# Loading q, k and v in blocks of sixteen subtiles, with three buffers each, and k's squared norms back on TensorE

## The chip, the core and the metric

The kernel runs on one core of a Trainium2 chip. Five engines work side by side, each through its own instruction stream: PE (matrix multiplication), DVE (VectorE), ACT (ScalarE), POOL (GpSimd) and SP (SyncE, which here only starts DMAs). Sixteen DMA engines move data between HBM and the on-chip memory. The metric is the device time in microseconds of one launch; the median of three runs before the change is 270.2 us (270.14 to 270.89).

## What is computed

There are four batches of 6336 tokens with 256 channels each. Channel attention works over the channels: the Gram matrix of k and q over all tokens of a batch, with both normalized over the tokens, goes through a softmax, and v is multiplied by the result. A highway layer follows on the 25344 rows.

```python
B, N, C = (4, 6336, 256)
qn = q / (np.linalg.norm(q, axis=1, keepdims=True) + 1e-06)
kn = k / (np.linalg.norm(k, axis=1, keepdims=True) + 1e-06)
s = kn.transpose(0, 2, 1) @ qn / tau
s = s - s.max(-1, keepdims=True)
a = np.exp(s)
a /= a.sum(-1, keepdims=True) + 1e-09
x = (v @ a).reshape(B * N, C)
H = np.maximum(x @ w_h, 0.0)
T = 1.0 / (1.0 + np.exp(-(x @ w_t + b_t)))
out = (T * H + (1.0 - T) * x)
```

Inputs and output are float32 in HBM. The loads turn q, k and v into float16 on the way (so a byte written on chip stands for two bytes read), and the output is stored as float32.

## The kernel before

**Tiles.** Of a batch's 6336 rows, 48 subtiles of 128 rows are laid out so that each of the 128 partitions holds 48 successive rows; the 192 rows that remain are two subtiles of 96 rows, the tail. `CH = 8` subtiles make a chunk. A load brings one chunk of q, k or v: 8 subtiles, 8 KB in a row per partition in HBM (512 KB written on chip). There are six chunks and a tail per batch and input. `QK_BUFS = 5` and `V_BUFS = 5` tiles are kept for each of q, k and v. Output tiles also hold a chunk (`O_BUFS = 7`), and are stored a chunk at a time (1 MB).

**Stage 1** (`stage1`, lines 441 to 459) goes over a batch's subtiles of q and k. For each half of the channels it issues a 128x256 matmul k'q (line 453), a 128x128 matmul k'k (line 455) and a 128x128 matmul q'q (line 457); the diagonals of the last two are the squared norms. All add up in two PSUM banks, `sg0` and `sg1`. In batches 1 to 3, for the first `APART = 5` chunks of q and the first `APART_K = 1` chunk of k, the 128x128 matmul is left out (lines 454 and 456). There ACT squares the tile (`squares`, two instructions of four subtiles, line 472), POOL adds the squares up in three or four steps (`sum_squares`, lines 478 to 489), PE sums them over partitions (line 524), DVE copies the sums (line 528) and adds them to the diagonals (line 612).

**The chain** (`plan_chain`) follows stage 1 of a batch: diagonals on DVE (line 575), the power -0.5 on POOL (line 586), scaling, exponentials on ACT (line 652), transposes, and a product with the two weight matrices folded into it (line 698). It leaves the float16 matrices `mr`.

**Stage 2** goes over pairs of subtiles, 25 a batch and 100 in all, counted by g. A pair of v is transposed on PE (line 769, or line 763 in the last batch) and copied out by ACT or DVE (lines 539 and 541). Then come three products of four 128x256 matmuls each (line 809): h for the first layer, t for the gate, d for x. ACT takes relu (line 849) and tanh (line 863), copies the bias into t (line 539, or DVE at line 541), and DVE combines them (lines 870 and 889). In the last batch, from chunk `BY_DMA = 3` on, v is transposed by DMA instead, on SP's queue (`transpose_chunk`, line 777).

**Order.** No loop writes the instructions in order. Each piece of work is added as a task to `Plan` (lines 92 to 226) with an engine, a key, estimated costs and the tasks it depends on; `run` plays the tasks through and issues on each engine the ready task with the smallest key. So the order on each engine is fixed when the program is built, and the chip then follows it, waiting by semaphores. Keys are pair numbers g plus an offset by kind and stage from `PRIO`. Stage 1 of batch b+1 is spread over the pairs of batch b by `slot_of` with `HEAD` and `ENDS`. Loads are issued by POOL, in the fixed order of `seq` (lines 407 to 418), where `V_AHEAD` shifts those of v; a load is issued once a buffer is free, and POOL's additions go ahead of a load when both can go. `loads_stop` keeps loads off POOL while it is needed for the chain's power. At most eight loads are under way. Transposes by DMA have the key g - `AHEAD`.

**Stores** go out by SP in chunks. A store is held until a later chunk, `LAG = 5` chunks on, has its first result (`plan_holds`, lines 930 to 940: a 1 KB DMA into `held_row` waits for that result and the store is queued behind it); from pair `UNTIL = 61` on they are not held.

The loads of batch 0's q and k come first: chunks 0 to 3 whole, chunk 4 in two halves, chunk 5 in pieces of 4, 2 and 2 subtiles. The first chunk of batch 1, the weights and the first chunk of v follow.

```python
def drops(nm, b, s):
    if s < S and s % CH == CH - 1:
        return [(ld[(nm, b, s // CH)][0], nm)]
```

This is what gives a load's tile back: its last subtile's use.

Of the kernel before, what the change touches and what calls it, by code (L numbers as in the profile page):

```python
# [16 lines left out]
CH = 8  # L17
QK_BUFS = 5
V_BUFS = 5
O_BUFS = 7  # L20
LAG = 5
UNTIL = 61
AHEAD = 16
# [4 lines left out]
APART_K = 1  # L28
V_AHEAD = -3
# [3 lines left out]
    "tr": (-13.858, 5.164, -69.544, 4.416),  # L33
    "ev": (116.624, 56.093, 133.515, 109.473),
    "h": (-52.706, -43.549, -42.913, -10.323),
    "bias": (25.973, -17.497, 24.705, 39.419),
    "t": (22.848, -15.916, 56.403, 18.956),
    "relu": (-70.319, -81.16, 27.028, -53.997),
    "x": (-78.578, -45.936, -122.371, -23.396),
    "gate": (-39.338, -48.519, -69.153, -40.842),  # L40
    "prod": (16.639, 6.587, 21.565, -25.923),
    "res": (-18.603, 23.463, -13.022, -57.01),
    "s1": (92.914, 52.821, 130.881),
    "sq": (-18.222, 44.489, 8.075),
}
POW = 0.75
HEAD = 6
TAIL = 63
EV = BIAS = ("ACT", "DVE")
ENDS = [20.75, 51.5, 67.25]  # L50
# [179 lines left out]
def kernel(  # L230
# [19 lines left out]
    NJ = S // CH  # L250
    TR = (N - P * S) // 2
# [16 lines left out]
        "sqq": 2, "sqk": 2, "vT": 3, "vT_t": 1, "o": O_BUFS, "ot": 1, "uu": 3, "pp": 3, "vtsb": 9, "mr0": 2, "mr1": 2,  # L268
# [49 lines left out]
    def load(nm, b, j, s, n):  # L318
        src = src_of[nm][b]
        if j == NJ:  # L320
            t = new(f"tail_{nm}", [P, 2, C], f16, f"{nm}{b}_t")
            tiles[(nm, b, j)] = t
            nc.gpsimd.dma_start(out=t[0:TR, :, :], in_=tail_rows(src))
            return
        if s == 0:
            tiles[(nm, b, j)] = new(nm, [P, CH, C], f16, f"{nm}{b}_{j}")
        t = tiles[(nm, b, j)]
        nc.gpsimd.dma_start(  # L328
            out=t[:, s : s + n, :], in_=main_rows(src)[:, j * CH + s : j * CH + s + n, :]
        )  # L330

    def sub(nm, b, s):

        if s < S:
            return tiles[(nm, b, s // CH)][:, s % CH, :]
        return tiles[(nm, b, NJ)][0:TR, s - S, :]
# [6 lines left out]
    def plan_load(nm, b, j, s=0, n=CH):  # L343

        size = P * n * C * 4 if j < NJ else TR * 2 * C * 4
        tag = nm if j < NJ else f"tail_{nm}"
        x = plan.add(
            "POOL", len(plan.tasks), 0.54, 0, [], lambda: load(nm, b, j, s, n),
            take=[tag] if s == 0 else [], size=size * (1 if j < NJ and n > 2 else SHORT),
        )  # L350
        ld.setdefault((nm, b, j), []).append(x)
        x.first = s

    def loaded(nm, b, s):

        if s >= S:
            return [ld[(nm, b, NJ)][0]]
        return [[x for x in ld[(nm, b, s // CH)] if x.first <= s % CH][-1]]

    def drops(nm, b, s):  # L360

        if s < S and s % CH == CH - 1:
            return [(ld[(nm, b, s // CH)][0], nm)]
        if s == NS - 1:
            return [(ld[(nm, b, NJ)][0], f"tail_{nm}")]
        return []

    plan_load("q", 0, 0)
    plan_load("k", 0, 0)
    consts = plan.add("POOL", len(plan.tasks), 0.6, 1.5, [], constants)  # L370
    consts.serial = True
    for j in range(1, NJ - 2):
        plan_load("q", 0, j)
        plan_load("k", 0, j)
        if j == 2:
            for nm in "qk":
                plan_load(nm, 0, NJ)
            b_ld = [
                plan.add("POOL", len(plan.tasks), 0.54, 0, [], lambda u=u: load_b(u), size=4000)
                for u in range(2)  # L380
            ]
    for j, s, n in ((NJ - 2, 0, 4), (NJ - 2, 4, 4), (NJ - 1, 0, 4), (NJ - 1, 4, 2), (NJ - 1, 6, 2)):
        plan_load("q", 0, j, s, n)
        plan_load("k", 0, j, s, n)
# [11 lines left out]
    plan_load("v", 0, 0)  # L396
# [11 lines left out]
    for b in range(B):  # L408
        for j in range(NJ + 1):
            if (b, j) != (0, 0):  # L410
                seq.append((NP * b + CH // 2 * j - V_AHEAD, 1, "v", b, j))
            if b >= 1 and (b, j) != (1, 0):
                at = slot_of((b - 1) * NS + CH * j)
                seq.append((at, 0, "q", b, j))
                seq.append((at, 0, "k", b, j))
    seq.sort(key=lambda x: (x[0], x[1]))
    for _, _, nm, b, j in seq:
        plan_load(nm, b, j)
# [4 lines left out]
    def natural(b):  # L423

        return b == B - 1 and BY_DMA <= NJ
# [5 lines left out]
    def order_of(b):  # L431

        if b:
            return list(range(NS))
        return [*range(3 * CH), *range(S, NS), *range(3 * CH, S)]
# [5 lines left out]
    def stage1(b, s):  # L441
# [8 lines left out]
        for c in range(2):  # L450
# [3 lines left out]
            if not apart("k", b, s // CH):  # L454
                nc.tensor.matmul(sg[c][:, C : C + P], kc, kc, start=False, stop=False)  # L455
            if not apart("q", b, s // CH):
# [6 lines left out]
    def apart(nm, b, j):  # L463
        return b > 0 and j < {"q": APART, "k": APART_K}[nm]
# [4 lines left out]
    def squares(nm, b, j, half):  # L469
        sq_t[nm, b, j, half] = sq = new("sq" + nm, [P, CH // 2, C], f32, f"sq{nm}{b}_{j}_{half}")  # L470
        x = tiles[(nm, b, j)][:, half * CH // 2 : (half + 1) * CH // 2, :]
        nc.scalar.activation(out=sq, in_=x, func=Act.Square)  # L472

    def sum_squares(nm, b, j, step):
        add = partial(nc.gpsimd.tensor_tensor, op=AluOp.add)
        if step == 0:
            sq, other = sq_t[nm, b, j, 0], sq_t.pop((nm, b, j, 1))
            add(out=sq, in0=sq, in1=other)  # L478
        elif step == 1:
            sq = sq_t[nm, b, j, 0]  # L480
            add(out=sq[:, 0:2, :], in0=sq[:, 0:2, :], in1=sq[:, 2:4, :])
        else:
            sq = sq_t.pop((nm, b, j, 0))
            if j == 0:
                sums[nm, b] = small.tile([P, C], f32, tag=f"sums{nm}", name=f"sums{nm}{b}")
                add(out=sums[nm, b], in0=sq[:, 0, :], in1=sq[:, 1, :])
            else:
                add(out=sq[:, 0, :], in0=sq[:, 0, :], in1=sq[:, 1, :])
                add(out=sums[nm, b], in0=sums[nm, b], in1=sq[:, 0, :])

    def plan_squares(nm, b):

        ends, x = {}, None
        for j in range({"q": APART, "k": APART_K}[nm]):
            key = slot_of((b - 1) * NS + CH * j) + PRIO["sq"][b - 1] + (nm == "k")
# [3 lines left out]
                    "ACT", key, 0.97, 1.07, loaded(nm, b, CH * j + CH // 2 * n),  # L499
                    lambda j=j, n=n: squares(nm, b, j, n), take=["sq" + nm],  # L500
# [5 lines left out]
                "POOL", key, 2.36, 2.45, parts, lambda j=j: sum_squares(nm, b, j, 0), drop=[(parts[1], "sq" + nm)]  # L506
            )
            y = plan.add("POOL", key, 1.27, 1.35, [y], lambda j=j: sum_squares(nm, b, j, 1))
            x = plan.add(
                "POOL", key, 1.3 if j else 0.65, 1.4 if j else 0.75, [y] + ([x] if x else []),  # L510
                lambda j=j: sum_squares(nm, b, j, 2), drop=[(parts[0], "sq" + nm)],
# [3 lines left out]

        def over_partitions():
            sums[nm, b, "ps"] = ps = new("vt", [P, 2], f32, f"sumps{nm}{b}")
            for c in range(2):
                x = sums[nm, b]
                if nm == "q" or natural(b):  # L520
                    x = x[:, bass.ts(c, P)]
                else:
                    x = x.rearrange("p (w two) -> p two w", two=2)[:, c, :]
                nc.tensor.matmul(ps[:, c : c + 1], x, ones[:, 0:1], start=c == 0, stop=c == 1)

        def keep():
            sums[nm, b, "sb"] = sb = small.tile([P, 2], f32, tag=f"sumsb{nm}", name=f"sumsb{nm}{b}")
            nc.vector.tensor_copy(out=sb, in_=sums[nm, b, "ps"])
# [14 lines left out]
    def plan_chain(b, own, last, key, apart_sums):  # L543
# [65 lines left out]
        def rest_of(nm, n):  # L609
            if b:  # L610
                x = st["x"][:, n : n + 2]
                nc.vector.tensor_tensor(out=x, in0=x, in1=sums[nm, b, "sb"], op=AluOp.add)

        dq = dve(
            lambda: (diagonal(0), diagonal(1), rest_of("q", 0)), 0.9, 0.95, [last, consts] + apart_sums[:1]
        )
        nq = pool(lambda: norm(0), POW, POW + 0.2, [dq])
        dk = dve(
            lambda: (diagonal(2), diagonal(3), rest_of("k", 2)), 0.9 if b else 0.75, 0.95 if b else 0.8,
            [dq] + apart_sums[1:],  # L620
        )
# [149 lines left out]
    def transpose_chunk(b, j):  # L771
# [4 lines left out]
        src = tiles[("v", b, j)][0:nr, :, :].rearrange("p s c -> p (s c)")  # L776
# [168 lines left out]
    def plan_stage1(b):  # L945
        x, own = None, []
        part_ends, apart_sums = {"q": {}, "k": {}}, []
        if b:
            for nm in "qk":
                part_ends[nm], z = plan_squares(nm, b)  # L950
                apart_sums.append(z)
        for n, s in enumerate(order_of(b)):
            key = -100 + n if b == 0 else slot_of((b - 1) * NS + s) + PRIO["s1"][b - 1]
            deps = loaded("q", b, s) + loaded("k", b, s) + ([x] if x else [])
            away = [nm for nm in "qk" if apart(nm, b, s // CH)]
            x = plan.add(
                "PE", key, 0.44 - 0.11 * len(away), 0.66, deps, lambda s=s: stage1(b, s),
                take=[sg_tag(b, n)] if n < 2 else [],
                drop=[z for nm in "qk" if nm not in away for z in drops(nm, b, s)],
            )  # L960
            x.lat = x.pitch if n < NS - 1 else 0.66
            if s % CH == CH - 1:
                for nm in away:
                    plan.add("NONE", 0, 0, 0, [x] + part_ends[nm][s // CH], None, drop=drops(nm, b, s))
            if n < 2:
                own.append((x, sg_tag(b, n)))
        ready[b] = plan_chain(b, own, x, -50, apart_sums)
# [142 lines left out]
```

## Time and profile before

| | |
|---|---|
| median of three runs | 270.2 us (270.14 to 270.89) |
| profiled execution: its own time | 270.2 us |
| its span, first to last instruction | 268.4 us |
| mean granted TensorE clock | 0.993 |
| matmuls on PE | 2395 records |
| loads of q, k and v | 28, 28 and 24, and 12 of tails |
| HBM read and written | 78.38 MB and 25.95 MB |

A page gives busy time by engine, then 40 equal slices of the span (6.7 us each) with the busy share of each engine in tenths, the share of the DMA engines, and the rate in GB/s, counted in bytes written. PEclk is the granted clock in tenths. A chain of waits follows the last instruction back to what released it. Groups of instructions give line, engine, operation, operands and count, then busy time and the mean of one in ns, then the idle time of the engine before them and what ended it.

The rows that the change touches, from the groups by shape:

```profile
L455 PE MATMUL sg<-k 128*128 128x128 f16 x336 | 67.2, 222 | 0.0
L457 PE MATMUL sg<-q 128*128 128x128 f16 x144 | 32.0, 222 | 0.0
L472 ACT ACTIVATE sqk<-k 128x1024 f32<-128x1024 f16 x6 | 6.2, 1055 | 0.0
L478 POOL TENSOR_TENSOR sqk<-sqk,sqk 128x1024 f32<-128x1024 f32 x3 | 7.1, 2352 | 0.0
L481 POOL TENSOR_TENSOR sqk<-sqk 128x512 f32<-128x512 f32 x3 | 3.8, 1270 | 0.0
L486 POOL TENSOR_TENSOR sumsk<-sqk 128x256 f32<-128x256 f32 x3 | 2.2, 732 | 0.0
L524 PE MATMUL sumpsk<-ones,sumsk 128*128 128x1 f32 x12 | 1.6, 238 | 0.0
```

Matmuls are pipelined, so the 222 ns of one is its time through the engine and not the time between starts. The DMA issues, with KB written and the median time from issue to landing:

```profile
out_dram<-o SPq DMA_DIRECT2D x23, 1024.0 KB, 9.6
v<-in_v_dram POOLq DMA_DIRECT2D x24, 512.0 KB, 16.7
q<-in_q_dram POOLq DMA_DIRECT2D x21, 512.0 KB, 15.5
k<-in_k_dram POOLq DMA_DIRECT2D x21, 512.0 KB, 17.3
```

### The profile page before, as it was taken

To read this page: it belongs to the slowest core of one execution; us is meant where nothing else is said; L and a number is where in the kernel's file an instruction comes from. 1 tells how busy PE (TensorE), PEld (TensorE's weight loads), DVE (VectorE), ACT (ScalarE), POOL (GpSimd) and SP (SyncE) were. 2 spreads that over 40 slices of the span, in tenths; PEclk is the share of its full clock that TensorE was granted. 3 is DMA by queue.
4 is the path that set the end of the run, shared out by engine and by line. 5 is a ranking of instruction groups with operands and counts; after the bars stand their busy time and mean duration, and the time that the engine had idled before them with its cause. 6 is when DMAs were issued, how large, how long until landed. Compare 5 with 4: busy or idle time off the path is not lost.

```text
span 268.4 us, 6188 instructions
## 1 busy us (share of the span) xinstructions
PE 243.8 (91%) x2395; PEld 214.8 (80%) x2395; DVE 185.5 (69%) x392; ACT 198.3 (74%) x361; POOL 144.1 (54%) x176
## 2 busy tenths in 40 slices
PE   0687976999999999999999999999999999999990
PEld 0576853898999788999999789988898888888880
DVE  1000036637877887878867997886788988889993
ACT  1001018958978899889988898888879989999990
POOL 7233468997797456986587549976773000010000
PEclk9999999999999999999999999999999999999997
DMA  6999999999999999999999999999999999998994
GB/s 112 213 213 208 205 203 207 213 214 212 214 214 213 212 213 246 256 236 278 288 262 246 283 260 244 288 244 274 288 265 329 331 327 352 319 203 148 397 415 173
DMA packets 24527, 67.24 MB, mean 250 GB/s; under 512 B 9009, under 2 KB 11185, under 8 KB 21553
## 3 DMA queue, kind: packets, MB, share of 16 engines
q0 software_dynamic: 13472, 39.20, 74.7%
q1 hardware_dynamic: 11024, 27.64, 28.4%
q8 instruction: 19, 0.31, 0.4%
q14 instruction: 12, 0.09, 0.1%
HBM read 78.38 MB, written 25.95 MB: 389 GB/s over the span
## 4 chain that ended last, share of the span: by engine, by line
PE 75%; DMA 13%; DVE 4%; ACT 3%; POOL 2%; issue 1%; DVEq 0%; ACTq 0%; POOLq 0%
PE t L809 15%; PE h L809 15%; PE d L809 15%; PE sg L453 12%; DMA k<-in_k_dram 10%; PE vtps L769 6%; PE sg L455 6%; DMA v<-in_v_dram 2%; PE sg L457 2%; DVE pp L870 1%; PE t L840 1%; ACT uu L863 1%; ACT t L539 1%; DMA out_dram<-o 1%; PE ah L698 1%
## 5 line engine op out<-in xcount | busy, mean ns | idle before, releaser
L809 PEld LDWEIGHTS <-vtsb 128*128 128x128 f16 (+1 forms) x1044 | 99.7, 99 | 18.2 <-issue 5.0
L453 PE MATMUL sg<-q,k 128*128 128x256 f16 x384 | 79.3, 275 | 14.1 <-DMA k<-in_k_dram 14.1
L870 DVE SCALAR_TENSOR_TENSOR pp<-uu,d 128x512 f32<-128x512 f32 (+1 forms) x100 | 68.1, 683 | 26.0 <-PE d L809 13.4
L863 ACT ACTIVATE uu<-t 128x512 f32<-128x512 f32 (+1 forms) x100 | 59.4, 597 | 13.1 <-PE t L809 12.2
L455 PE MATMUL sg<-k 128*128 128x128 f16 x336 | 67.2, 222 | 0.0
L889 DVE SCALAR_TENSOR_TENSOR o<-h,pp 128x512 f32<-128x512 f32 x96 | 65.5, 685 | 1.5
L849 ACT ACTIVATE d<-h 128x512 f32<-128x512 f32 (+1 forms) x100 | 57.6, 581 | 6.3 <-PE h L809 4.9
L809 PE MATMUL t<-mr,vtsb 128*128 128x256 f16 (+1 forms) x348 | 52.0, 272 | 1.8 <-ACT t L539 1.7
L809 PE MATMUL h<-mr,vtsb 128*128 128x256 f16 (+1 forms) x348 | 52.1, 272 | 1.1 <-DVE vtsb L541 0.5
L453 PEld LDWEIGHTS <-k 128*128 128x128 f16 x384 | 37.7, 99 | 18.4 <-DMA k<-in_k_dram 15.5
L809 PE MATMUL d<-mr,vtsb 128*128 128x256 f16 (+1 forms) x348 | 51.8, 272 | 0.3 <-ACT d L849 0.2
L478 POOL TENSOR_TENSOR sqq<-sqq,sqq 128x1024 f32<-128x1024 f32 x15 | 35.5, 2364 | 20.5 <-ACT sqq L472 20.5
L539 ACT COPY t<-bias_all 128x512 f32<-128x512 f32 (+1 forms) x62 | 36.6, 590 | 1.5
L455 PEld LDWEIGHTS <-k 128*128 128x128 f16 x336 | 33.1, 99 | 0.9
L328 POOL DMA_DIRECT2D v<-in_v_dram x24 | 13.4, 559 | 35.6 <-DMA vT<-v 18.9
L457 PE MATMUL sg<-q 128*128 128x128 f16 x144 | 32.0, 222 | 0.0
L472 ACT ACTIVATE sqq<-q 128x1024 f32<-128x1024 f16 x30 | 31.0, 1051 | 0.0
L769 PE MATMUL vtps<-ident,v 128*128 128x128 f32 x144 | 27.7, 274 | 0.7 <-DMA v<-in_v_dram 0.7
L541 DVE COPY vtsb<-vtps 128x256 f32<-128x256 f32 (+2 forms) x55 | 22.9, 416 | 7.0 <-PE vtps L769 7.0
L575 DVE SCALAR_TENSOR_TENSOR junk<-sg,ident 128x128 f32<-128x128 f32 x16 | 4.6, 288 | 33.3 <-PE sg L457 32.7
L328 POOL DMA_DIRECT2D k<-in_k_dram x28 | 15.4, 549 | 9.6 <-DMA k<-in_k_dram 8.4
L328 POOL DMA_DIRECT2D q<-in_q_dram x28 | 15.6, 558 | 9.0 <-DMA q<-in_q_dram 7.3
(86 smaller groups left out, 267.7 us busy)
## 6 DMA issues: line engine op xcount, KB each, us to landing
out_dram<-o SPq DMA_DIRECT2D x23, 1024.0 KB, 9.6
v<-in_v_dram POOLq DMA_DIRECT2D x24, 512.0 KB, 16.7
q<-in_q_dram POOLq DMA_DIRECT2D x21, 512.0 KB, 15.5
k<-in_k_dram POOLq DMA_DIRECT2D x21, 512.0 KB, 17.3
q<-in_q_dram POOLq DMA_DIRECT2D x5, 256.0 KB, 9.8
k<-in_k_dram POOLq DMA_DIRECT2D x5, 256.0 KB, 9.1
out_dram<-o SPq DMA_DIRECT2D x2, 512.0 KB, 3.9
out_dram<-ot SPq DMA_DIRECT2D x4, 192.0 KB, 6.5
```

The source lines that it names most:

```text
L328: nc.gpsimd.dma_start(out=t[:, s : s + n, :], in_=main_rows(src)[:, j * CH + s : j * CH + s + n, :])
L453: nc.tensor.matmul(sg[c][:, 0:C], kc, qa, start=first, stop=False)
L455: nc.tensor.matmul(sg[c][:, C : C + P], kc, kc, start=False, stop=False)
L457: nc.tensor.matmul(sg[c][:, C + P : C + 2 * P], qa[:, cs], qa[:, cs], start=False, stop=last)
L478: add(out=sq, in0=sq, in1=other)
L539: nc.scalar.copy(out=out, in_=in_)
L769: nc.tensor.transpose(ps[:, u, 0:nr], v.bitcast(f32), ident0[0:nr, 0:nr])
L809: nc.tensor.matmul(out[0:nr, u, :], vt[u][kt][:, 0:nr], mr[kt][:, col * C : (col + 1) * C], **flags(u, kt))
L849: nc.scalar.activation(out=d[0:nr, :, :], in_=ps_t["h", b, i][0:nr, :, :], func=Act.Relu, scale=0.5)
L863: nc.scalar.activation(out=uu[0:nr, :, :], in_=ps_t.pop(("t", b, i))[0:nr, :, :], func=Act.Tanh, scale=-0.5)
L870: nc.vector.scalar_tensor_tensor(out=pp[0:nr, :, :], in0=el.pop(("uu", b, i))[0:nr, :, :], scalar=1.0, in1=ps_t.pop(("d", b, i))[0:nr, :, ...
L889: nc.vector.scalar_tensor_tensor(out=ot, in0=ps_t.pop(("h", b, i))[0:nr, :, :], scalar=0.0, in1=el.pop(("pp", b, i))[0:nr, :, :], op0=AluO ...
```

## The change

A load brings `LC = 16` subtiles, so a batch has three blocks and a tail per input, and each partition reads 16 KB in a row. There are three tiles for each of q, k and v. The work itself keeps its chunk of eight: sums of q's squares, output tiles, stores and transposes by DMA. A block's tile is given back when its sixteenth subtile has been used. Batch 0's q and k are still loaded eight subtiles at a time, up to the last block, which comes in pieces of 8, 4, 2 and 2; the first block of q and k of batch 1 comes as 4, 4 and 8, and that of v as 8 and 8. The tails of batch 0 are loaded and used after subtile 32, rather than 24.

The squares of k leave ACT and POOL: `APART_K` is gone, and line 455's matmul is issued for every subtile. q keeps its five chunks.

The numbers that place the work are others as well: `PRIO`, `HEAD`, `ENDS`, `UNTIL`, `AHEAD` and `V_AHEAD`. So the order on every engine changes. The counts that change on the engines: PE has 384 rather than 336 matmuls of k'k on whole subtiles, and 6 fewer sums over partitions. ACT has 6 squares fewer, 2 copies of `et`, 2 biases of the tail, 1 `mr` and 2 copies of `vtsb` more, which DVE has fewer. POOL issues 47 rather than 80 loads of q, k and v. SP has 11 rather than 10 holds.

```diff
 CH = 8
-QK_BUFS = 5
-V_BUFS = 5
+LC = 16
+QK_BUFS = 3
+V_BUFS = 3
 O_BUFS = 7
 LAG = 5
-UNTIL = 61
-AHEAD = 16
+UNTIL = 63
+AHEAD = 11
 BY_DMA = 3
...
 APART = 5
-APART_K = 1
-V_AHEAD = -3
+V_AHEAD = 2.5
...
-    "s1": (92.914, 52.821, 130.881),
-    "sq": (-18.222, 44.489, 8.075),
+    "s1": (2.894, 15.325, 6.393),
+    "sq": (-0.758, 4.066, 5.437),
 }
 POW = 0.75
-HEAD = 6
+HEAD = 4
 TAIL = 63
 EV = BIAS = ("ACT", "DVE")
-ENDS = [20.75, 51.5, 67.25]
+ENDS = [15.75, 46.75, 59.75]
...
+    NL = S // LC
...
         if s == 0:
-            tiles[(nm, b, j)] = new(nm, [P, CH, C], f16, f"{nm}{b}_{j}")
+            tiles[(nm, b, j)] = new(nm, [P, LC, C], f16, f"{nm}{b}_{j}")
         t = tiles[(nm, b, j)]
         nc.gpsimd.dma_start(
-            out=t[:, s : s + n, :], in_=main_rows(src)[:, j * CH + s : j * CH + s + n, :]
+            out=t[:, s : s + n, :], in_=main_rows(src)[:, j * LC + s : j * LC + s + n, :]
         )
...
-        if s < S and s % CH == CH - 1:
-            return [(ld[(nm, b, s // CH)][0], nm)]
+        if s < S and s % LC == LC - 1:
+            return [(ld[(nm, b, s // LC)][0], nm)]
...
+    for s, n in ((0, 8), (8, 4), (12, 2), (14, 2)):
+        plan_load("q", 0, NL - 1, s, n)
+        plan_load("k", 0, NL - 1, s, n)
...
-        return [*range(3 * CH), *range(S, NS), *range(3 * CH, S)]
+        return [*range(S - LC), *range(S, NS), *range(S - LC, S)]
...
-            if not apart("k", b, s // CH):
-                nc.tensor.matmul(sg[c][:, C : C + P], kc, kc, start=False, stop=False)
-            if not apart("q", b, s // CH):
+            nc.tensor.matmul(sg[c][:, C : C + P], kc, kc, start=False, stop=False)
+            if not apart(b, s // CH):
...
-        dk = dve(
-            lambda: (diagonal(2), diagonal(3), rest_of("k", 2)), 0.9 if b else 0.75, 0.95 if b else 0.8,
-            [dq] + apart_sums[1:],
-        )
+        dk = dve(lambda: (diagonal(2), diagonal(3)), 0.75, 0.8, [dq])
...
-        src = tiles[("v", b, j)][0:nr, :, :].rearrange("p s c -> p (s c)")
+        s = j * CH % LC
+        src = tiles[("v", b, j * CH // LC)][0:nr, s : s + n, :].rearrange("p s c -> p (s c)")
```

## The prediction

> **What bounds the kernel now.** I read the page, then the waits of PE, the timeline around first uses, and each load's landing.
>
> ```profile
> span 268.4 us, 6188 instructions
> ...
> PE 243.8 (91%) x2395; PEld 214.8 (80%) x2395; DVE 185.5 (69%) x392; ACT 198.3 (74%) x361; POOL 144.1 (54%) x176
> ...
> PE   0687976999999999999999999999999999999990
> ...
> DMA  6999999999999999999999999999999999998994
> GB/s 112 213 213 208 205 203 207 213 214 212 214 214 213 212 213 246 256 236 278 288 262 246 283 260 244 288 244 274 288 265 329 331 327 352 319 203 148 397 415 173
> ...
> PE 75%; DMA 13%; DVE 4%; ACT 3%; POOL 2%; issue 1%; DVEq 0%; ACTq 0%; POOLq 0%
> ```
>
> PE has almost no hole after 45 us, yet the DMA engines are full too, at 213 GB/s of float16 written until stores join at 101 us. Who waits?
>
> ```profile
> PE sg L453 <- DMA k<-in_k_dram: 14.1, 6, 8.9
> PE t L809 <- ACT t L539: 1.7, 4, 0.6
> PE vtps L769 <- DMA v<-in_v_dram: 0.7, 1, 0.7
> PE d L809 <- ACT d L849: 0.6, 2, 0.4
> PE h L809 <- DVE vtsb L541: 0.5, 1, 0.5
> PE h L809 <- DVE o L889: 0.5, 1, 0.5
> ```
>
> Columns: total, times, longest. The k waits lie in the first 41 us. Then PE waits 3.3 us for ACT and DVE. But PE meets its data just as they land:
>
> ```profile
> 62.42 0.27 PE L453 MATMUL sg<-q,k 128*128 128x256 f16 x1
> 62.53 0.22 PE L455 MATMUL sg<-k 128*128 128x128 f16 x1
> 62.59 0.27 PE L453 MATMUL sg<-q,k 128*128 128x256 f16 x1
> ```
>
> This is chunk 3 of batch 1; its k landed at 61.87 (the load's semaphore). The starts give pitches: 0.109 us for 256 columns, 0.056 for 128.
>
> I call the sum of pitches ahead of an instruction, in program order, its work position, and its start less that sum its lag. Lag grows only when PE idles. Before: 8.9 us at the first matmul, 20.6 at 62 us, 21.0 at 82, 22.4 at 128, 23.7 at 155, 25.0 at 183, 27.1 at the last. A load sets a floor under it: landing less position of first use. So far as 82 us the floors (k of chunks 1, 3 and 4: 49.54-30.0 = 19.5; 61.87-41.8 = 20.1; 69.43-49.0 = 20.4) lie within 0.6 us of the lag: DMA and PE bound together.
>
> **The change, part by part.** The sum is made against this execution, span 268.4, which is 270.2 us, 1.8 around it; the median is 270.2 too.
>
> *k's squares go back to PE.* 48 matmuls of 128x128 are added (8 subtiles x 2 halves x 3 batches): 48 x 0.056 = 2.7 us. The sums over partitions of k leave: the chain has q's twin at 0.46 us, three times 1.4. Net **+1.3 us**, all of it path, since nothing hides PE. Off go also 6 ACT squares (6 x 1.05 = 6.3 us) and three POOL chains (3 x 4.4 = 13 us). I count these as nothing: both engines have idle time (ACT 26%, POOL 46%). Bounds: -3.3, PE's waits on ACT and DVE, to 0; I take 0, since those waits (at 92, 151, 181 and 204 us) lie 12 us or more from any sum of k's squares (POOL's first steps start at 47, 106 and 163).
>
> *Loads of sixteen subtiles.* The bytes are the same; what moves is when a first use is allowed, since a whole load must land. The changed program's order gives positions. Its second q and k pair (subtiles 16 to 31 of batch 1) is first used at 39.6 us of work; its bytes have landed when, in the present kernel, chunk 3 has, as the same bytes stand ahead of both: 61.87. Floor 22.2, against 20.6 of lag now. Its third k is first used at 54.1 and ends with the bytes of chunk 5, 76.83: floor 22.8 against 20.9. v subtiles 32 to 47 of batch 0: first use 58.9; v chunk 5 landed at 87.65, less two tails and two k, q chunks now ahead of it (5.9), 81.75: floor 22.9 against 21.0. So PE loses 1.9 us here by waits for whole loads.
>
> *The larger row.* No load of this size is in the trace. Loads of 256 KB landed 1.24 us apart, of 512 KB 2.45: halving costs 1.2%. The packets' records, 327 ns for 4096 B and 173 for 2048, have 19 ns fixed, so 8192 B would be 2.9% quicker; the low bound is nothing gained, as 16 engines' packets overlap. I take 1.2%: six such loads by there, 29.4 us, give 0.35 (0 to 0.85). Lag **+1.5 us**. A rule speaks for much more: the Trainium skill, "DMA: Bandwidth & Descriptors", section "Anatomy of one DMA", gives each software-issued DMA 2.0 us fixed besides its bytes. There are 33 loads of q, k and v fewer, which would be 66 us. The row shows 512 KB loads landing 2.45 us apart, some six in flight (15.5 to 17.3 us from issue to landing), so the fixed part is hidden.
>
> *Does the lag stay?* Later floors: k of the last third of batch 2, first use 105.7, ends with bytes that landed at 130.4 (132.86 less one v chunk), less 0.6 for larger rows: 24.1, against 22.4+1.5. That adds **0.2**. v of batch 2, first use 132.0: 157.84-0.95-132.0 = 24.9 against 23.7+1.7, no more. k of the last third of batch 3, first use 159.5: (188.36-2.45-1.0)-159.5 = 25.4 against 25.0+1.7. Were the waits in between all taken up by the early one, this last floor would leave 0.4 of 1.7. With nothing from larger rows the early floor gives 1.9 and the one at 105.7 (24.7 against 24.3) 0.4 more. So 0.4 to 2.3.
>
> *Three buffers.* POOL issues loads in order past its sums; a load needs its tile free. The tightest early one, q of batch 2, needs q of batch 1 done at position 35.2, near 58 us, and its turn on the DMA comes at 82. Cover 24 us: nothing. v's last third of batch 3 waits for position 193.4, some 221 us, and is needed by transposes only.
>
> *Transposes by DMA move on SP's queue.* AHEAD falls from 16 to 11: the first, now issued at 222.2 and landed at 235.6, goes behind two stores that wait for pair 74 (near 230). By today's 13.4 us it lands at 243; PE wants it at position 217.9, lag 28.3: 246. Cover 3 us; if gone, it costs what it is late, and behind it are the stores of batch 3 on SP.
>
> *Tail.* Before, the last matmuls are d of pair 99, and DVE ends 2 us later. After, pair 98's d comes just ahead of them, so two more DVE operations (0.69 each), less the 0.44 and some overlap, stand behind: **+0.6** (0 to 1.2).
>
> Sum: 1.3 + 1.5 + 0.2 + 0.6 = 3.6; 270.2 + 3.6 = **273.8 us**. With the bounds of these terms and up to 1.5 us of new waits in the other order of ACT and DVE, its own range is 272.0 to 276.5.
>
> **Rivals.**
> *Lighter ACT and DVE take the later waits away* (faster). From 82 us on lag grows by 6.1 us, at the ends of batches' chains and in the last pairs. ACT has 6.3 us less to do. If over 4.4 of the 6.1 vanish, 273.8 falls under 269.4; all of it, with no floor, 267.7. Against: the floor of 25.4, worked out above, lets the end fall to 270.2+1.3+0.6-1.7 = 270.4, or 269 if rows are 2.9% quicker.
>
> *A new wait at the end* (slower still): the transposes, 3 us of cover, or v's 1 MB loads, which share the DMA with a later flush of stores (from pair 62 rather than 58). Each chunk late by 3 us gives 276.8. For: SP's order. Against: there is less load traffic left then than now, DMA falls to 203 GB/s and lower at 235 us.
>
> *The rows change nothing and the early floors are soft:* the lag of 1.7 us is taken up by waits that would have come anyhow, 270.2+1.3 and the last floor's 0.4 plus 0.6 of tail less today's waits of 1.5 on ACT: 271.0, no change.
>
> **How the numbers follow.** Forecast 0.69; slower by the end, 0.11; nothing, 0.10; faster, 0.10. What can be told from no change here is 0.3%, 0.8 us, so faster is under 269.4, slower over 271.0. The forecast and the late rival are slower: 0.80; 0.10 same, 0.10 faster. The range: the forecast's own, down to 270.4 where the last floor puts an end to absorption, and up to 277.8 for a chunk a little over 3 us late: 270.4 to 277.8.
>
> **What would show it.** PE waits on DMA for k and v between 55 and 85 us, where today are none; lag 22.5 rather than 21.0 at position 60; 1 MB loads landing 4.8 to 4.9 us apart; 384 matmuls of sg from k alone; PE's idle on ACT and DVE near 3 us still; transposes not waited for. I would be wrong if PE entered batch 1 at today's lag, if 1 MB loads landed under 4.76 apart, or if vT were waited for.

## The result, and the profile after

| | before | after |
|---|---|---|
| median | 270.2 us (270.14 to 270.89) | 273.6 us (273.38 to 274.37, four runs) |
| ratio to before, 95% interval | | 1.0125 [1.01, 1.0151] |
| profiled execution: its own time, its span | 270.2, 268.4 us | 273.5, 271.7 us |
| mean granted TensorE clock | 0.993 | 0.995 |

The kernel is slower by 3.4 us, where 3.6 was forecast (273.8). The page of the changed kernel, with the lines that answer to those of before:

```profile
span 271.7 us, 6186 instructions
...
PE 246.5 (91%) x2431; PEld 216.6 (80%) x2431; DVE 184.1 (68%) x379; ACT 196.1 (72%) x362; POOL 116.8 (43%) x138
...
PE 71%; DMA 13%; ACT 5%; DVE 5%; issue 2%; POOL 2%; DVEq 0%; ACTq 0%; POOLq 0%
...
L457 PE MATMUL sg<-k 128*128 128x128 f16 x384 | 75.7, 222 | 0.0
```

PE is busy 2.7 us longer in a span 3.3 us longer. POOL is relieved by 27 us and ACT by 2, and the kernel is slower all the same. In the chain of waits PE's share falls from 75% to 71%, and ACT and DVE together rise from 7% to 10%: PE now waits for others a little more. What it waits for (total, times, longest):

```profile
PE sg L456 <- DMA k<-in_k_dram: 13.5, 7, 8.9
PE t L806 <- ACT t L538: 1.5, 4, 0.8
PE vtps L765 <- DVE vtsb L540: 1.4, 2, 1.0
PE ah L694 <- DVE o L886: 0.6, 1, 0.6
PE d L806 <- ACT d L846: 0.5, 2, 0.3
```

The total for k is no larger than before (14.1), but two of its waits are new, and they lie behind 50 us, where before PE waited for no load at all. The timeline of PE in the changed kernel, with a few rows around them (start, duration, engine and line, tiles, shape, count, and in brackets the idle time before and what ended it):

```profile
50.03 0.28 PE L456 MATMUL sg<-q,k 128*128 128x256 f16 x1 [0.41 <-DMA k<-in_k_dram]
...
57.48 0.60 PE L806 MATMUL t<-mr,vtsb 128*128 128x256 f16 x4 [0.28 <-ACT t L538]
...
58.26 0.60 PE L806 MATMUL d<-mr,vtsb 128*128 128x256 f16 x4 [0.19 <-ACT d L846]
...
61.57 0.28 PE L456 MATMUL sg<-q,k 128*128 128x256 f16 x1 [0.54 <-DMA k<-in_k_dram]
```

Between 54.9 and 61.5 us PE has no stage 1 at all: the second block of k has not landed. It runs stage 2 alone, and there ACT does not keep up. Busy time by stretch shows it, first of the kernel before, then of the changed one (stretch, its length, busy us and instructions of PE, PE's weight loads, DVE, ACT and POOL, then clock, DMA share, GB/s):

```profile
55.00:60.00 5.00, 4.99 (x56) 4.46 (x54) 1.69 (x4) 1.69 (x4) 4.60 (x4) 1.00 1.05 211
60.00:65.00 5.00, 4.96 (x50) 4.33 (x48) 3.83 (x7) 4.72 (x8) 2.97 (x6) 1.00 1.07 215
```

```profile
55.00:60.00 5.00, 4.23 (x35) 3.16 (x34) 3.62 (x6) 4.49 (x10) 4.55 (x5) 1.00 1.04 218
60.00:65.00 5.00, 4.38 (x44) 3.61 (x43) 1.94 (x4) 4.19 (x7) 3.08 (x3) 1.00 1.04 216
```

PE loses 0.76 and 0.58 us here, and with them the lag of the prediction (start less work position) goes from 19.0 at position 30 to 22.9 at position 57, against 20.2 and 21.0 before. The last half microsecond of the 22.9 comes while PE runs stage 2 ahead of the third block of k, and not from a wait for it: the block landed at 76.19 us and is first used at 76.97.

```profile
75.03 0.38 PE L765 MATMUL vtps<-ident,v 128*128 128x128 f32 x2
75.47 0.60 PE L806 MATMUL t<-mr,vtsb 128*128 128x256 f16 x4
75.94 0.44 PE L765 MATMUL vtps<-ident,v 128*128 128x128 f32 x2
76.53 0.60 PE L806 MATMUL h<-mr,vtsb 128*128 128x256 f16 x4 [0.16 <-DVE o L886]
76.97 0.27 PE L456 MATMUL sg<-q,k 128*128 128x256 f16 x1
```

From start to start the two pairs of transposes take 0.44 and 0.59 us, where their pitches add up to 0.22; by the profile ACT's `t` ended the first delay and DVE's `o` the second. After position 57 the lag grows by 6.1 us to the last matmul in both kernels.

Position counts the added matmuls as work, so the wall clock must decide what they cost. Start of the first h matmul of the last pair of each batch, from PE's timeline:

| | before | after | difference |
|---|---|---|---|
| batch 0 | 109.53 | 111.39 | 1.86 |
| batch 1 | 170.04 | 172.19 | 2.15 |
| batch 2 | 223.02 | 225.85 | 2.83 |
| batch 3 | 260.60 | 264.10 | 3.50 |

More than half of the loss is there by the end of batch 0. The rest comes in small steps, in two traces whose orders differ.

### The profile page after: what moved, and what is told of

It reads as the page before. It is cut to its first block, busy times and chain, and to the rows that moved or that the text cites. A ratio compares the mean times of both kernels' runs of the same rounds, so it can differ in the third digit from the quotient of the medians.

```text
span 271.7 us, 6186 instructions
## 1 busy us (share of the span) xinstructions
PE 246.5 (91%) x2431; PEld 216.6 (80%) x2431; DVE 184.1 (68%) x379; ACT 196.1 (72%) x362; POOL 116.8 (43%) x138
## 4 chain that ended last, share of the span: by engine, by line
PE 71%; DMA 13%; ACT 5%; DVE 5%; issue 2%; POOL 2%; DVEq 0%; ACTq 0%; POOLq 0%
PE t L806 15%; PE h L806 14%; PE d L806 14%; DMA k<-in_k_dram 13%; PE sg L456 11%; PE sg L457 6%; PE vtps L765 5%; DVE pp L867 2%; PE sg L459 2%; ACT uu L860 2%; ACT sq L475 1%; ACT t L538 1%; PE t L837 1%; DVE o L886 1%; PE vtps L759 1%
## 5 line engine op out<-in xcount | busy, mean ns | idle before, releaser
L456 PE MATMUL sg<-q,k 128*128 128x256 f16 x384 | 81.8, 275 | 13.5 <-DMA k<-in_k_dram 13.5
L457 PE MATMUL sg<-k 128*128 128x128 f16 x384 | 75.7, 222 | 0.0
L846 ACT ACTIVATE d<-h 128x512 f32<-128x512 f32 (+1 forms) x100 | 58.2, 585 | 4.8 <-PE h L806 4.1
L456 PEld LDWEIGHTS <-k 128*128 128x128 f16 x384 | 37.8, 99 | 17.9 <-DMA k<-in_k_dram 15.3
L481 POOL TENSOR_TENSOR sq<-sq,sq 128x1024 f32<-128x1024 f32 x15 | 35.5, 2364 | 37.5 <-ACT sq L475 37.4
L538 ACT COPY t<-bias_all 128x512 f32<-128x512 f32 (+1 forms) x64 | 37.7, 590 | 1.6
L457 PEld LDWEIGHTS <-k 128*128 128x128 f16 x384 | 37.9, 99 | 1.1
L475 ACT ACTIVATE sq<-q 128x1024 f32<-128x1024 f16 x30 | 30.7, 1049 | 0.0
L540 DVE COPY vtsb<-vtps 128x256 f32<-128x256 f32 (+2 forms) x53 | 22.1, 418 | 7.3 <-PE vtps L765 6.7
L765 PEld LDWEIGHTS vtps<-ident,v 128*128 128x128 f32 x144 | 17.1, 141 | 3.9 <-DVE vtsb L540 2.3
L484 POOL TENSOR_TENSOR sq<-sq 128x512 f32<-128x512 f32 x15 | 19.2, 1282 | 0.9
```

What stands on the lines that cost most here:

```text
L456: nc.tensor.matmul(sg[c][:, 0:C], kc, qa, start=first, stop=False)
L475: nc.scalar.activation(out=sq, in_=qa, func=Act.Square)
L538: nc.scalar.copy(out=out, in_=in_)
L765: nc.tensor.transpose(ps[:, u, 0:nr], v.bitcast(f32), ident0[0:nr, 0:nr])
L846: nc.scalar.activation(out=d[0:nr, :, :], in_=ps_t["h", b, i][0:nr, :, :], func=Act.Relu, scale=0.5)
```

## Experiments

All ratios are to the kernel before, run on the same chip; its medians there were 270.76, 270.83 and 270.38 us. An edited kernel's line numbers are shifted by a few lines.

**1. The matmuls of k by k in the kernel before.** First the move of the squares alone, in the old order:

```diff
-            if not apart("k", b, s // CH):
+            if True:
                 nc.tensor.matmul(sg[c][:, C : C + P], kc, kc, start=False, stop=False)
     def squares(nm, b, j, half):
+        if nm == "k":
+            return
...
```

(and the same for POOL's sums of k, its sums over partitions and their copy).

> The kernel before, in its order, with k's squares of the first chunk on PE and its ACT squares, POOL sums and sums over partitions gone. If PE is the path: 48 x 0.056 - 3 x 0.46 = 1.3 us more, 271.5. If what ACT and POOL are spared shortens the waits after the softmax chains: under 271, down to 268.2 (PE's 3.3 us of waits on ACT and DVE).

Measured: 271.95 us, ratio 1.0044 [1.0029, 1.0058], which is 1.2 us (0.8 to 1.6), as the first term has it. Then the 48 matmuls with nothing taken away, so that only the first edit above is made:

> The kernel before in its own order with the same 48 matmuls added and nothing taken away (k's squared norms of batches 1 to 3 count the first chunk twice in the output). Moving the squares back to PE took 1.2 us there. If the matmuls count in full, as the prediction's first term has it, 2.7 us more than the kernel before, 272.9 on its 270.2. If a part of them fits into the waits ahead of the first chain (3.0 us for k's landings between positions 22.8 and 23.8), about 1.8.

Measured: 272.24 us, ratio 1.0071 [1.0057, 1.0084], 1.9 us (1.5 to 2.3) of the 2.7, near the second figure. In the trace, taken of a run of 272.62 us, less is hidden: the lag is 0.8 us under that of the kernel before at position 25, as the waits ahead of the first chain shrink, but only 0.3 at position 57 and 0.15 at the end. So most of this work counts here, and between 0.2 and 0.8 us of it does not.

**2. The same matmuls in the changed kernel.** Left out, in its own order (k's squared norms of batches 1 to 3 then lack the first eight subtiles):

```diff
-            nc.tensor.matmul(sg[c][:, C : C + P], kc, kc, start=False, stop=False)
+            if not (b and s < CH):
+                nc.tensor.matmul(sg[c][:, C : C + P], kc, kc, start=False, stop=False)
```

> The changed kernel, in its order, without the 128x128 matmuls k'k of the first eight subtiles of batches 1 to 3 (k's squared norms then miss those rows). If the added PE work is path from end to end, 48 x 0.056 = 2.7 us go: 273.6 - 2.7 = 270.9. If the landing of the second k block (61.5 us) sets PE's start there, the 16 matmuls ahead of it (0.9 us) only make PE wait longer: 271.8. If the added work was hidden: 273.6.

Measured: 273.81 us, ratio 1.0114 [1.0095, 1.0134]. The loss is 3.1 us (2.6 to 3.6), where that of the changed kernel is 3.4 (2.7 to 4.1). So 2.7 us less of work on PE gains nothing clear of noise, and 1.2 us at most. Then the same matmuls twice (`for _ in range(2 if b and s < CH else 1)` around the call):

> The changed kernel in its own order; each of the 48 matmuls of k by k that the change brought back (first eight subtiles of batches 1 to 3) is issued twice, so k's squared norms count that chunk twice in the output: 2.7 us more of PE work at the places where leaving it out gained nothing. If PE's work there is on the path, 2.7 us more, 276.3. If it lies in holes that landings and the chains of ACT and DVE leave, as leaving it out suggested, 1 us or less, 274.6 or below. Between the two: the holes were about filled by what the change added.

Measured: 274.32 us, ratio 1.0152 [1.013, 1.0174]: 2.7 us more of work cost some 0.7 (-0.2 to 1.6 by the intervals). So in the changed kernel these matmuls fill holes for the most part, and most of what they added is not on the path.

Where do the holes close? The waits of PE without the matmuls, then with twice the matmuls:

```profile
PE sg L456 <- DMA k<-in_k_dram: 12.4, 4, 8.9
PE t L807 <- ACT t L539: 1.8, 5, 0.8
PE cqb L634 <- DVE dcat L600: 1.4, 1, 1.4
PE vtps L766 <- DVE vtsb L541: 1.4, 2, 1.0
PE ah L695 <- DVE o L887: 0.9, 1, 0.9
```

```profile
PE sg L456 <- DMA k<-in_k_dram: 13.1, 6, 9.0
PE t L807 <- ACT t L539: 1.5, 4, 0.8
PE vtps L766 <- DVE vtsb L541: 1.4, 2, 1.0
```

The first eight subtiles of a batch are what PE does while the chain of the batch before runs on DVE, POOL and ACT. Without their k'k, PE stands longer for `dcat` and for DVE's work ahead of `ah`; with twice as much, neither wait is left (the rows not shown are of 0.5 us or less; the changed kernel itself stands 0.5 us for `dcat` and 0.6 for `ah`). Not all of the 1.4 us for `dcat`, in batch 0's chain, is due to the matmuls: in this execution the granted clock was 0.50 from 25.8 to 29.2 us, and three runs of the third experiment with such a drop and all their matmuls stood 0.98 us there. The drop does not hide a gain in the time: of the four runs two have a mean clock of 0.987 and two of 0.994 and 0.996, and all lie between 273.77 and 273.94 us. Batch 2's chain, in the stretch from 158 to 164 us: without the matmuls, in the changed kernel, and with twice as many.

```profile
158.00:164.00 6.00, 4.84 (x39) 3.69 (x38) 5.93 (x14) 3.96 (x11) 4.72 (x4) 1.00 1.03 249
```

```profile
158.00:164.00 6.00, 5.44 (x52) 4.57 (x51) 5.93 (x14) 4.28 (x12) 4.43 (x4) 1.00 1.02 246
```

```profile
158.00:164.00 6.00, 6.00 (x67) 5.59 (x65) 5.33 (x15) 4.07 (x11) 5.26 (x5) 1.00 1.04 239
```

In the first two DVE is full (5.93 of 6), and `ah` of batch 2 starts at 163.5 and 163.3 us: the added matmuls change PE's busy time and not the moment. Only in the third is PE itself full.

**3. What holds PE between 55 and 67 us.** Three things could: the landing of the second block of k, ACT, or the landing of v. First the block of k in two halves, with the order on PE, ACT and DVE kept; five later loads are issued a little behind their places, so that POOL's sums keep theirs:

```diff
+            for at in (0, CH) if (nm, b, j) == ("k", 1, 1) else (s,):
+                m = CH if (nm, b, j) == ("k", 1, 1) else n
                 nc.gpsimd.dma_start(
-                    out=t[:, s : s + n, :], in_=main_rows(src)[:, j * LC + s : j * LC + s + n, :]
+                    out=t[:, at : at + m, :], in_=main_rows(src)[:, j * LC + at : j * LC + at + m, :]
                 )
...
```

> The changed kernel with its own order on every engine but POOL; only the second block of k of batch 1 is loaded in two halves (ahead of it the block of q), and five later loads are issued a little behind their places so that POOL's sums keep theirs. Its first half then lands about 59.1 us instead of 61.5. Theory (the whole block of k is waited for, and the wait stays to the end): the 0.70 us wait of PE at 60.8 us goes, lag 22.2 instead of 22.9 at position 57, 272.9 us where the changed kernel takes 273.6. Rival 1 (the order laid around the late block sets the pace through ACT, and PE's wait for k only fills what ACT would take): the lag at position 57 falls by 0.3 or less. Rival 2 (what is won there is given back at later landings): lag 22.2 at position 57 and 273.6 us at the end.

Measured: 273.76 us, ratio 1.0108 [1.0083, 1.0133]. The half landed early, and PE's wait at 61.57 was gone: lag 21.1 at position 40. At position 45 it was 22.2 again, as in the changed kernel. The wait that took its place:

```profile
63.40 0.60 PE L820 MATMUL t<-mr,vtsb 128*128 128x256 f16 x4 [0.80 <-ACT t L552]
```

Then less work for ACT, with the block whole:

```diff
     def squares(b, j, half):
+        if (b, j) == (1, 1):
+            return
...
```

> The changed kernel in its own order; ScalarE's squares of the second chunk of q of batch 1 (2 x 1 us at 51.8 us) and GpSimd's four sums of them are left out, so q's squared norms of batch 1 lack one chunk in the output. Theory (the landing of the second block of k at 61.5 us is the floor): PE's 1.4 us of waits on ACT between 55 and 60 us go, PE then stands for k until 61.5 instead, about 2.1 us in place of 0.7, lag at position 57 still 22.9, 273.6 us. Rival (ACT's work sets the time in this stage): lag at position 57 1 us or more lower, 272.5 us or less.

Measured: 273.74 us, ratio 1.0108 [1.0081, 1.0135]. PE's waits for ACT's `t` fall to 0.1 us each, and it stands for k until 61.58 just the same; lag 22.9 at position 57, as the theory had it. But the wait for k was 0.56 us where 2.1 was expected: without ACT's waits PE had other short ones, for DVE's `t` and for ACT's `d`. Both edits:

> Both edits at once: the second block of k of batch 1 in two halves, and the squares of the second chunk of q of batch 1 with their sums left out (q's squared norms of batch 1 lack that chunk in the output). Theory: both causes of PE's holes between 55 and 61 us are gone, so lag 20.8 to 21.3 at position 57, as in the kernel before (21.0); if that is kept to the end, 271.6 us; if the later landings take it back, 273 us or more with lag back at 24 by position 105. Rival (neither was the cause): lag 22.5 or more at position 57.

Measured: 273.59 us, ratio 1.01 [1.0076, 1.0124], lag 22.8 at position 57: the rival, with the same 0.80 us for ACT at 63.41. ACT's squares of the third chunk stood at 59.7, ahead of the evictions that PE needed. So these went too:

> As the run with both edits (second block of k of batch 1 in two halves, squares of the second chunk of q of batch 1 left out), and ScalarE's squares of the third chunk of q of batch 1 (2 us at 59.7 us, ahead of the evictions that PE waited for at 63.4 us) with GpSimd's sums are left out too, so q's squared norms of batch 1 lack two chunks in the output. Theory (in a stretch of stage 2 alone, ScalarE paces PE, and its squares in that stretch are what PE stands for): the 0.8 us wait at 63.4 us goes, lag at position 45 21.2 to 21.4 instead of 22.1, and since waits early in the kernel are kept, 272.7 us. Rival (the next wait takes its place once more): lag at position 57 22.7 or more and 273.6 us.

Measured: 273.88 us, ratio 1.0124 [1.011, 1.0138], lag 22.8 at position 57. The rival once more. In this kernel PE waits for the next load:

```profile
66.89 0.44 PE L783 MATMUL vtps<-ident,v 128*128 128x128 f32 x2 [0.52 <-DMA v<-in_v_dram]
```

So three marks stand at nearly the same lag. In the changed kernel they are the landing of k's block, 61.52-39.6 = 21.9; the eviction that pair 6 waits for, 63.4-41.3 = 22.1; and the landing of v's second block, 66.41-44.8 = 21.6, or 22.0 in the last kernel, where it landed 0.4 us later. Taking one or two of them away shows the next one and gains nothing that lasts: the last pair of batch 0 stood at 111.39, 111.63, 111.38, 111.37 and 111.57 us in the changed kernel and these four. None of the four lifts v's mark, and the three with the split block set it later: v's second block landed at 66.89, 66.68 and 66.84 us, for a reason that was not looked for. So half a microsecond of gain by the first two marks may be hidden there; all three marks lie above 21.0, the lag before.

**4. A late landing alone.** In the kernel before, the second load of k of batch 1 was issued behind the third of q:

```diff
+        if (nm, b, j) == ("k", 1, 1):
+            return
+        for x, i in (("q", 2), ("k", 1)) if (nm, b, j) == ("q", 1, 2) else ((nm, j),):
...
```

> The kernel before in its own order; only the second load of k of batch 1 is issued behind the third of q instead of ahead of it, so that it lands about 2.45 us later, near 52.0 us, as a part of a longer load would. It is the landing floor by itself: wanted at position 30.0, floor 22.0 against a lag of 20.2, so PE waits about 1.8 us for it. Theory (a wait for a landing early in the kernel stays to the end, which is what the prediction's +1.5 rests on): 1.5 to 1.9 us more than the kernel before, 272.0 on its 270.2. Rival (the later growth of lag absorbs it): within 0.4 us of the kernel before.

Measured: 273.41 us, ratio 1.0096 [1.0062, 1.013], 2.6 us. The timeline of PE and its stretches show why it is more than 1.9:

```profile
52.82 0.28 PE L456 MATMUL sg<-q,k 128*128 128x256 f16 x1 [2.39 <-DMA k<-in_k_dram]
...
54.34 1.06 PE L812 MATMUL d<-mr,vtsb 128*128 128x256 f16 x4
```

```profile
53.00:54.00 1.00, 1.00 (x10) 0.83 (x9) 0.00 (x0) 0.00 (x1) 1.00 (x3) 0.74 1.07 213
54.00:55.00 1.00, 1.00 (x8) 0.76 (x7) 0.00 (x0) 0.97 (x2) 1.00 (x3) 0.50 1.04 209
55.00:56.00 1.00, 1.00 (x6) 0.74 (x5) 0.50 (x1) 0.22 (x1) 0.06 (x1) 0.50 1.11 221
56.00:58.00 2.00, 2.00 (x19) 1.68 (x16) 0.88 (x2) 1.72 (x3) 0.00 (x0) 0.78 1.05 213
```

The wait is 2.4 us, and half a microsecond later the granted clock falls to 0.50; a group of four matmuls takes 1.06 us, where the rows of the changed kernel above have 0.60. The clock costs 0.26+0.50+0.50+0.44 = 1.7 us more. In the trace, the lag is 4.3 us above that of the kernel before from position 34 on, and 4.3 at the last matmul: nothing of it is absorbed. The six runs lie at 272.6 to 272.7 (three) and 274.1 to 274.8 (three); the profiled one is of the second group, and 1.7 us between them is what the clock costs in the trace. That the first group kept its clock is an inference, as no trace of one was taken; the mean granted clocks of its runs, 0.992 to 0.998 against 0.986 to 0.991 in the second, speak for it. That group is 1.8 us over the kernel before, within the theory's 1.5 to 1.9.

**5. Smaller loads in place of whole blocks.** Every block of sixteen issued as two loads of eight, the changed kernel's order kept on PE, ACT and DVE:

```diff
+        if n == LC and nm == "q":
+            return
+        for at in (0, CH) if n == LC else (s,):
+            for x in "qk" if n == LC and nm == "k" else nm:
...
```

> The changed kernel with the same order on PE, ACT and DVE; only each load of sixteen subtiles is issued as two of eight, q and k in turns. If what PE loses is its waits for whole blocks, the wait for k at 60.8 us (0.7, and 0.25 just behind it) goes: 272.7. If all of the early lag (1.9 us) were such waits: 271.7. If block size has no part in it: 273.6, or more by eight to sixteen further issues on POOL (0.55 us each, off the path).

Measured: 291.76 us, ratio 1.0777 [1.0757, 1.0797]; none of the expectations. POOL's timeline:

```profile
54.68 0.53 POOL L333 DMA_DIRECT2D q<-in_q_dram  x1 [1.91 <-DMA q<-in_q_dram]
57.12 0.53 POOL L333 DMA_DIRECT2D k<-in_k_dram  x1 [1.92 <-DMA k<-in_k_dram]
57.66 2.35 POOL L486 TENSOR_TENSOR sq<-sq,sq 128x1024 f32<-128x1024 f32 x1
```

Most loads here are issued only when an earlier one has landed, and POOL stands 1.9 us in front of each. Its first sum of squares starts at 57.66 us, where the changed kernel has it at 45.12. Only two tiles hold squares, so ACT stands, and PE stood 13.7 us for ACT's `t`. The loads' issue, not their landing, made this time; it says nothing of the forecast's terms.

So the order was laid anew, with all loads of eight:

```diff
-            s = CH if (b, j) == (0, 0) else 0
-            seq.append((NP * b + (LC * j + s) // 2 - V_AHEAD, 1, "v", b, j, s))
+            for s in (0, CH) if j < NL else (0,):
+                if (b, j, s) != (0, 0, 0):
+                    seq.append((NP * b + (LC * j + s) // 2 - V_AHEAD, 1, "v", b, j, s))
...
```

> The changed kernel with tiles of sixteen, but loads of eight, each with its own due time, so that the order is laid anew with the same keys. If blocks cost mainly through the order (pairs of stage 2 in a row while a block is awaited, which ACT cannot keep up with: 1.4 us of waits on ACT at 55 to 60 us) and through the wait for k (0.9), lag at position 57 falls from 22.9 to about 21 and the time to 271.7. If the new keys are what costs, 273 or more.

Measured: 278.0 us, ratio 1.0267 [1.025, 1.0284]. The lag is 21.3 at position 57, 1.6 under the changed kernel's, as expected, and stays 1.3 to 3.3 under it up to position 180. The last pair of batch 0 comes at 110.63, 0.8 ahead of the changed kernel. From position 185 on it rises from 25.8 to 32.6 at the last matmul: another order of the last batch, in which PE waits in many small pieces. Then halves for batch 1's q and k and batch 0's v alone:

> The changed kernel's tiles, buffers and sort keys (v's lead 3 instead of 2.5), with loads of eight subtiles for q and k of batch 1 and v of batch 0 only, loads of sixteen after that, and the order laid anew by the planner. Theory (blocks of sixteen cost 1.6 us, all of it before position 57, because the work that a block feeds is ordered around its late landing): lag about 21.2 at position 57 and, if the planner's order of batches 2 and 3 is as good as the changed kernel's, 272.0 us. Rival (the order of the later batches decides by itself): lag 21.2 at position 57 and 273 us or more, with waits on ACT and DVE behind position 185.

Measured: 277.55 us, ratio 1.026 [1.0246, 1.0274]. Lag 21.4 at position 57, 25.8 at position 80, 33.2 at the end: the rival. The waits that did it lie at the end of batch 1's stage 1 and in the chain behind it:

```profile
91.62 0.60 PE L809 MATMUL t<-mr,vtsb 128*128 128x256 f16 x4 [0.87 <-ACT t L541]
...
96.68 0.67 PE L636 MATMUL cqb<-dcat,ones 128*128 128x256 f32 x2 [1.25 <-DVE inv L594]
```

Both laid a new order, from sort keys chosen for other loads. In both the early gain of smaller loads is there, and more than it is lost behind. No kernel of this study beat the kernel before.

## Why the prediction was right, and where not

*Blocks of sixteen, lag +1.5.* The place is right, and the mechanism in part. The second block of k landed at 61.52 us and was waited for; the working gave 61.87 less 0.35. But the 22.5 was the floor of two later loads, and these were not waited for: the third block of k landed at 76.19 and v's third at 81.05, floors of 22.1 and 22.2. The lag at position 57 to 60 is 22.9, 0.7 above any floor, and 1.9 above the kernel before where 1.5 was taken. The one landing that was waited for stands for 0.9 of this (21.9 against 21.0); the rest came behind it, from ACT and DVE at 63 and 75 to 77 us, which the forecast had only in its range. PE's two waits for k are a smaller part of it (0.9 us), because the order was laid around the late block and hands PE a stretch of stage 2 alone that ACT cannot feed. And it is not one mark but three within 0.5 us of lag: the third experiment removed two of them without gain. The fifth shows the size from the other side: with the same sort keys, loads of eight and the order they lead to, the lag there is 1.6 us less. Lifting v's mark, or all three, in the changed kernel's own order was not tried.

*k's squares, +1.3, "all of it path, since nothing hides PE".* This is the step that failed. In the kernel before it is right (1.2 us measured), and of the matmuls alone most counts. In the changed kernel it is wrong: the matmuls left out gain nothing clear of noise, doubled they cost some 0.7. They stand behind marks that are set in wall time, the landings up to 67 us and DVE's work at the batches' ends. Adding position and lag made the sum come out, since a lag under a fixed mark shrinks as position grows: with the matmuls left out the last lag is 32.0 rather than 29.0. So the blocks and their new order alone cost 3.1 of the 3.4 us (ratio 1.0114), and the two terms overlap instead of adding up. That the forecast fell within 0.2 us of the result is luck in part. In its own terms, too, errors offset each other: the lag of the last matmul is some 2 us above that before, where 1.7 was forecast, and the tail is 0.2 us shorter, where 0.6 longer was.

*Larger rows, 1.2%.* The six from 52 to 81 us landed 4.84 to 4.94 us apart, mean 4.88, against twice 2.45: 0.5%. The bound of nothing was nearer. That k's block landed just 0.35 us early, as worked out, is in part chance: the weights, ahead of any load of sixteen, had landed 0.29 us earlier than before (41.87 and 42.16). The profile counts 51 loads of q, k and v after, not 47, so 29 fewer than before and not 33. The Trainium skill ("DMA: Bandwidth & Descriptors", "Anatomy of one DMA") gives each software-issued DMA a fixed cost of about 2.0 us. Added up over 29 loads that would be 58 us, an estimate. The landings show none of it: split in two, k's block landed its halves 2.46 and 2.51 us apart.

*The floor at 105.7, +0.2.* It did not bind. Its load landed at 124.97 us, where the working had about 129.8: a floor of 19.3 against a lag of 24.1.

*ACT and POOL relieved, 0.* It fits the kernel before, where the move of the squares cost 1.2 us with both engines relieved, against 1.3 for PE's work alone. In the changed kernel it was not taken apart. The rival that it takes the later waits away falls: behind position 57 the lag grows by 6.1 us in both kernels. PE's waits for ACT and DVE, which were to stay near 3 us, are 5.7 by the page, 2.2 of them in the chain of batch 0 ahead of 47 us.

*Does the lag stay?* One late landing in the kernel before stays to the end in full (fourth experiment), more strongly than the forecast held.

*Three buffers and transposes.* No cover was used up. The first transpose by DMA was queued at 230.83 and took at most 11.6 us to land; PE used it at 246.4. At least 4.0 us of cover are left, 3 were worked out.

*Tail, +0.6.* Wrong: from the last d to the end of the span it is 6.3 us after and 6.5 before. In the kernel before the d of the last pair but one also stood just ahead of the last, 0.96 us, which the working overlooked.

Three things stay open. The small steps of loss behind batch 0 (2.15 to 3.50 us in the table) were not taken apart. How much of the 3.1 us is the loads' and how much the new sort keys' is not shown, as loads of sixteen under the old keys were not run. And with other sort keys a planned order might keep the 1.6 us of smaller loads; that was not searched.

## What to carry to other kernels

A wait for a landing is a mark in wall time. Work of another engine ahead of it costs nothing until it fills the hole, so the two must not be added up; leave one out at a time, and double it, before calling either the path. When a load is made larger, look for everything that the new landing feeds and everything ordered around it: several marks can stand close together, and removing one shows only the next.

In a kernel whose order is laid out by a planner, an edit that makes it plan anew changes every batch. Hold the order fixed, as most experiments here did, and check that queued issues still fit: twice as many loads on a queue that also carries sums cost 18 us.

## What the runs showed of the hardware

A short wait can cost nearly twice its length. A PE wait of 2.39 us took the granted clock to 0.50 for some 3.4 us, 1.7 us more. In batch 0 of other runs waits of 1.95 to 2.21 us did the same, but waits of 1.92 to 2.23 us in others did not. The length alone does not decide:

```profile
24.45 0.28 PE L468 MATMUL sg<-q,k 128*128 128x256 f16 x1 [1.97 <-DMA k<-in_k_dram]
```

```profile
24.50 0.28 PE L456 MATMUL sg<-q,k 128*128 128x256 f16 x1 [1.97 <-DMA k<-in_k_dram]
```

The first is PE in the last kernel of the third experiment; from 25 to 28 us its clock was 0.50. The second is PE in the changed kernel with the matmuls doubled, where the clock stayed at 1.00.

What tells them apart in the 14 traces is where the wait lies. Within every trace the times at which the granted clock switches are whole multiples of 3.41 us apart (14.77, 25.01 and 28.43 us in the run with less work for ACT). Cut a trace into stretches of 3.41 us from its first switch on. The clock is 0.50 behind every stretch in which PE stood for 1.95 us or more in all, and 1.00 behind every one in which it stood for 1.82 us or less. The first wait above lies within one stretch (21.30 to 24.71 us); the second is split at 24.17 us into 1.64 and 0.33. Where the stretches begin differs from run to run, and that would give a late landing two groups of times, as in the fourth experiment. All this is read from the traces; no experiment moved a wait across such a border.

The Trainium skill, "TensorE: Matmul & The Clock Gate", section "Why this matters for your kernels", asks for no idle gaps of PE over about 3 us between bursts of matmuls. These rows are stricter: a gap of 2.0 to 2.4 us was enough where it lay within one stretch. In batch 0 the later landings took the loss back, lag 0.8 higher at position 25 and equal at position 36; at 53 us nothing did.
